# A SwiGLU second layer in 26 bilinear products instead of Strassen's 28, with hidden rows summed per four f tiles

## The chip, the core and the metric

One core of one Trainium2 chip runs the whole kernel. The metric is the device time of one execution in microseconds (us), median over runs; lower is better. All inputs and the output are fp32.

The engines in the text are TensorE (PE, matrix products), VectorE (DVE), ScalarE (ACT), GpSimd (POOL) and SyncE (SP, which here only issues DMAs). Each engine works through its own list of instructions strictly in order. POOL and SP both issue DMAs from such a list.

## The reference, cut

S = 2048 tokens, D = 1024, F = 3584, 32 heads of 32.

```python
xn = layernorm(x)
q, k, v = split_heads(xn @ wqkv)
phi = lambda t: where(t > 0, t + 1, exp(t)) + 1e-6
kv, z = einsum("bhsd,bhse->bhde", phi(k), v), phi(k).sum(s)
o = (phi(q) @ kv) / (phi(q) . z + 1e-6)
s = o @ wo
h = silu(xn @ w1) * (xn @ w3)            # 2048 x 3584
out = x + s * silu(h @ w2)               # w2 is 3584 x 1024
```

## The kernel before

**Products.** Every large product is cut into 2 x 2 blocks and computed with Strassen's 7 products of sums of blocks (`PRODUCTS`, L69). Each fp32 operand is split into a high and a low part (`split`, L92: ACT makes the high part at L96, DVE the low part at L97), and `mm3` (L101) multiplies a pair with three matmuls of 128x512 on L104 to L106.

**Stages.** The tokens are taken in two halves of 1024, h = 0 and h = 1. In each half come keys and queries, then the hidden layer: 14 pairs of f tiles (`half`, L785; one f tile is 128 of the 3584 columns), each with a gate and an up product (`gemm`, L547), 168 matmuls per pair. After the second half the attention product `attention` (`Segment`, L1146) makes s = o @ wo with a merged weight `wp`, in eight token groups m = 0..7, and stores s. Then the second layer h @ w2 follows (`Layer`, L1246) in five blocks of f (`FB`), its results added up in SBUF in `acc`, with silu, the multiplication by s and the addition of x in `finish` (L1402).

**Hidden rows.** `use_gate` (L874) puts silu(gate) into a 2 KB tile `sg`; `use_up` (L878) multiplies by up on DVE (L880) and stores the rows of h with a POOL DMA (L884). `sums` (L888) makes the four sums of blocks that Strassen needs for its left operands, with four POOL additions of 128x256 (`four_sums`, L863 to L867) per token chunk, into tiles `hs`, and stores them (L892) from POOL in h = 0 and from SP in h = 1. The `sg` tiles come from a pool of four places (`psg`), the `hs` tiles from `pc`.

**Jobs.** Side work is written as generators in a list `jobs`. `catch_up` (L530) advances the first of them by one step, at about six places per `gemm`; what is left when the hidden layer is issued is then run to its end (`for j, _ in jobs: run(j)` in `half`). Jobs use four shared 4 KB places (`job_tile`, L125). In h = 0 the jobs are `prepare_next` and 23 of the 28 sums of second-layer weights (`weight_sums`, L905: load 512 KB of w2, four POOL additions of 128x256 on L899 to L903, store to `wt_d`). In h = 1 the remaining five sums run on DVE during keys and queries, then `attention_work` (L1110): the divided queries `qd`, the merged weights `wp`, and more divisions.

**Into the attention product.** The first token group's raw left operands (`left`, L1328, with `first=True`) are put in job places: `r0q`, `r2q`, `r4q`, `r6q`, two operands each, loaded by SP from `qs_d` and split on ACT and DVE into `XA11s`, `XS2s` and so on. PE's first attention matmul, `B11s<-wp,XA11s`, needs the first of them.

The order of instructions on each engine is set by the framework's scheduler when the kernel is compiled. Names in the rows below: `h1_13_1` is the h tile of half 1, pair 13, second f tile; `hs1_6_20` holds sums of half 1, quad 6, product 20; `w2_5_1` is the loaded weight block of quad 5, column part 1, and `w2s5_1_0` the first tile of its sums. `DMAHW` and `DMASW` are lanes of SP's and POOL's DMA queues; a DMA that waits for a lane waits for the last DMA on it. The number at the end of each name counts buffers.

## Time and profile before

| what | value |
|---|---|
| time, three runs | 2308.01, 2309.46 (median), 2310.02 us |
| span of the profiled execution | 2307.8 us |
| median less span | 1.66 us |
| granted TensorE clock over the span | 1.000 |
| first matmul of the attention product, last of the hidden layer (they interleave) | 1611.68 and 1615.08 us from the span's start |
| first matmul of the second layer | 1768.39 us |
| busy share: PE, DVE, ACT, POOL | 99%, 77%, 40%, 27% |

The rows of a profile give, for each engine, source line and shape, how many instructions there were, how long they were busy and what the engine waited for before them. POOL's 27% is a mean over the span: it is busy in the two hidden stages and almost idle after 1640 us.

### The profile page before, as it was taken

Reading aid. Unit: us, or ns where it says so; the run is one execution under the profiler, and the core shown is the slowest. Engines: PE = TensorE matmul, PEld = TensorE weight load, DVE = VectorE, ACT = ScalarE, POOL = GpSimd, SP = SyncE. Lnnn points to the kernel's source line nnn. Section 1 sums busy time; section 2 is a strip of 40 time slices with the busy share of each in tenths; the row PEclk is TensorE's granted clock in tenths of the full one; section 3 lists DMA queues with packets and bytes.
Section 4 is the critical chain, followed back from the end, with each engine's and each line's share of the span. In section 5 each row is a group of like instructions: output and inputs, shape, how many; then the busy total and the mean of one; then the engine's idle time right before and its main releaser. Section 6 shows DMA issues by size and latency. Waiting matters only on the chain.

```text
span 2307.8 us, 31551 instructions
## 1 busy us (share of the span) xinstructions
PE 2285.8 (99%) x10752; PEld 1875.1 (81%) x10752; DVE 1769.3 (77%) x2870; ACT 927.4 (40%) x1653; POOL 624.3 (27%) x779
## 2 busy tenths in 40 slices
PE   7999999999999999999999999999999999999998
PEld 6888888888888887777888888888888888888887
DVE  8987888897876775667867788887745676767697
ACT  6555443423332555433333433334324634243443
POOL 2220524286854211001423345342310000000011
PEclk9999999999999999999999999999999999999999
DMA  6555556576659656886756667665756544654488
GB/s 238 182 181 177 184 170 192 164 242 210 215 182 333 214 178 215 274 255 195 225 183 191 192 196 213 203 213 167 239 171 194 160 141 139 197 158 149 147 272 255
DMA packets 346657, 461.90 MB, mean 200 GB/s; under 512 B 23184, under 2 KB 261776, under 8 KB 346384
## 3 DMA queue, kind: packets, MB, share of 16 engines
q1 hardware_dynamic: 311488, 348.72, 48.3%
q0 software_dynamic: 35008, 111.18, 15.0%
q8 instruction: 84, 1.38, 0.3%
q14 instruction: 77, 0.63, 0.1%
HBM read 297.27 MB, written 166.20 MB: 201 GB/s over the span
## 4 chain that ended last, share of the span: by engine, by line
PE 94%; DVE 3%; DMA 2%; issue 0%; ACT 0%; SPq 0%; DVEq 0%; ACTq 0%
PE aB L106 3%; PE aB L105 3%; PE aB L104 3%; PE g L104 2%; PE g L105 2%; PE g L106 2%; PE dB L106 2%; PE dB L105 2%; PE dB L104 2%; PE cB L105 1%; PE bB L105 1%; PE cB L106 1%; PE bB L106 1%; PE bB L104 1%; PE cB L104 1%; PE trk L645 1%
## 5 line engine op out<-in xcount | busy, mean ns | idle before, releaser
L884 POOL DMA_DIRECT2D h_d<-sg x112 | 82.6, 738 | 286.7 <-DVE sg L880 264.8
L1415 POOL DMA_DIRECT2D out<-acc x14 | 7.9, 562 | 484.7 <-DVE acc L1414 476.9
L97 DVE TENSOR_TENSOR xy<-xy,xy 128x512 fp32r<-128x512 f32 x112 | 72.9, 686 | 63.7 <-ACT xy L96 63.7
L1259 DVE TENSOR_TENSOR acc<-aB,acc 128x512 f32<-128x512 f32 x111 | 73.5, 687 | 57.3 <-PE aB L106 57.3
L96 ACT CAST xy<-xy 128x512 fp32r<-128x512 f32 x112 | 65.0, 620 | 101.5 <-PE g L106 62.1
L105 PE MATMUL g<-xy,xy 128*128 128x512 f32 x224 | 87.6, 391 | 0.2 <-DVE xy L97 0.2
L106 PE MATMUL g<-xy,xy 128*128 128x512 f32 x224 | 87.2, 390 | 0.0
L104 PE MATMUL g<-xy,xy 128*128 128x512 f32 x224 | 82.6, 398 | 0.0
L649 POOL DMA_DIRECT2D y_d<-y x48 | 34.6, 723 | 125.7 <-ACT y L673 70.4
L866 POOL TENSOR_TENSOR hs<-sg 128x256 f32<-128x256 f32 x56 | 59.7, 1065 | 0.0
L864 POOL TENSOR_TENSOR hs<-hs,sg 128x256 f32<-128x256 f32 x56 | 58.9, 1051 | 0.1
L1259 DVE TENSOR_TENSOR acc<-dB,acc 128x512 f32<-128x512 f32 x56 | 38.5, 688 | 21.1 <-PE dB L106 20.6
L104 PEld LDWEIGHTS g<-xy,xy 128*128 128x128 f32 x224 | 41.8, 188 | 14.2 <-issue 3.7
L867 POOL TENSOR_TENSOR hs<-sg,hs 128x256 f32<-128x256 f32 x56 | 51.0, 911 | 1.6
L1383 POOL DMA_DIRECT2D s_d<-s x32 | 17.3, 541 | 121.9 <-DVE s L1190 69.2
L863 POOL TENSOR_TENSOR hs<-sg,sg 128x256 f32<-128x256 f32 x56 | 49.6, 887 | 1.2
L105 PEld LDWEIGHTS g<-xy,xy 128*128 128x128 f32 x224 | 42.0, 188 | 9.7 <-DVE xy L97 1.0
L1028 POOL DMA_DIRECT2D qs_d<-qd x32 | 18.1, 564 | 115.9 <-DVE qd L1024 82.4
L106 PEld LDWEIGHTS g<-xy,xy 128*128 128x128 f32 x224 | 42.0, 188 | 8.8
L892 POOL DMA_DIRECT2D h_d<-hs x60 | 46.4, 774 | 3.9 <-POOL hs L867 2.4
L96 ACT CAST XA12B<-rA12B 128x384 fp32r<-128x384 f32 (+1 forms) x40 | 19.8, 494 | 63.4 <-PE aB L106 54.6
L805 POOL DMA_DIRECT2D pq_d<-pq x32 | 17.5, 548 | 99.0 <-DVE pq L639 98.9
(5327 smaller groups left out, 8196.2 us busy)
## 6 DMA issues: line engine op xcount, KB each, us to landing
h_d<-hs POOLq DMA_DIRECT2D x60, 256.0 KB, 3.1
h_d<-sg POOLq DMA_DIRECT2D x56, 256.0 KB, 3.7
w<-in_B_w SPq DMA_DIRECT2D x56, 256.0 KB
wt_d<-w SPq DMA_DIRECT2D x28, 512.0 KB
xy<-x_d SPq DMA_DIRECT2D x28, 512.0 KB
xy<-y_d SPq DMA_DIRECT2D x28, 512.0 KB
h_d<-hs SPq DMA_DIRECT2D x52, 256.0 KB
y_d<-y POOLq DMA_DIRECT2D x48, 256.0 KB, 3.2
```

What stands on the lines that cost most here:

```text
L96: nc.scalar.copy(out=hi, in_=src)
L97: return nc.vector.tensor_sub(out=lo, in0=src, in1=hi.bitcast(F32))
L104: nc.tensor.matmul(acc, lhsT=wh, rhs=ah, start=start, stop=False, skip_group_check=True)
L105: nc.tensor.matmul(acc, lhsT=wh, rhs=al, start=False, stop=False, skip_group_check=True)
L106: return nc.tensor.matmul(acc, lhsT=wl, rhs=ah, start=False, stop=stop, skip_group_check=True)
L863: e.tensor_add(out=s1, in0=a21, in1=a22)
L864: e.tensor_sub(out=s2, in0=s1, in1=a11)
L866: e.tensor_sub(out=s3, in0=a11, in1=a21)
L867: e.tensor_sub(out=s4, in0=a12, in1=s2)
L884: nc.gpsimd.dma_start(out=h_d[i][2 * h + c][:, 2 * n:4 * n + 2, k], in_=src)
L892: queue.dma_start(out=h_d[i][2 * h + c][:, 6 + 4 * e:10 + 4 * e, k], in_=o[e].rearrange("p (e s) -> p e s", s=P))
L1259: nc.vector.tensor_add(out=c[t, n], in0=src, in1=c[t, n])
```

## The change

**Second layer.** Instead of 28 products for a 4 x 4 x 2 block scheme (Strassen four times over) there are 26 (`CHAINS`, `TAKES`), over all of f at once: f is cut into 4 groups of 7 tiles, tokens into 4 tiles per chunk of 512, the output into 2 halves. Products that go to neighbouring outputs are chained in one PSUM bank. A step is one product and one token chunk: 104 steps of 7 f tiles x 3 = 21 matmuls of 128x512. Signs are carried by `NEGATED` right operands. The right operands are sums of four blocks of w2.

**Hidden sums.** The rows of h are now summed per quad of four f tiles. `early_sums` (after an even pair) issues 7 POOL additions or subtractions and 6 DMAs, `later_sums` (after an odd pair) 21 and 10, all of 128x256 elements. They are generators in `hsums`, one step per `catch_up`. All their DMAs are issued by POOL. The last quad's sum tiles are job places.

**Weight sums.** There are still 28 tasks, now one per quad t and column part, with 11 POOL operations each: 7 on 128x256 elements and 4 on 128x128. A task uses three job places (the loaded block `r`, and `o1`, `o2`) and three stores. 16 tasks run in h = 0; the other 12 are on POOL in h = 1, appended to the jobs behind `attention_work`, instead of five on DVE during keys and queries.

**Places.** Ten shared 4 KB places (`pb`) take the operands, the h tiles and the raw left operands, in place of eight of 4 KB and four of 2 KB.

The diff, cut:

```diff
+    CHAINS = [[7], [23, 6, 0], [21, 20, 18, 19], [10, 8, 3], [1, 25, 17], [24, 4, 13, 12], [22, 11, 16, 5], [14, 15, 9, 2]]
...
-    pb = era2.enter_context(tc.tile_pool(name="pb", bufs=8, side="right"))
-    psg = era2.enter_context(tc.tile_pool(name="psg", bufs=4, side="right"))
+    pb = era2.enter_context(tc.tile_pool(name="pb", bufs=10, side="right"))
...
     def catch_up(*marks):
 
+        if hsums and next(hsums[0], done) is done:
+            hsums.pop(0)
...
-            jobs.append((last_weight_sums(), True))
...
         jobs.append((attention_work(), False) if h else (next_work(), True))
+        if h:
+            jobs.append((last_weight_sums(), False))
...
         for j, _ in jobs:
             run(j)
         jobs.clear()
+        if h:
+            for j in hsums:
+                run(j)
+            hsums.clear()
...
         def use_up(n, c, src):
-            nc.vector.tensor_mul(out=sg[n, c], in0=src, in1=sg[n, c])
...
+            a = tiles[2 * odd + n][:, c]
+            nc.vector.tensor_mul(out=a, in0=src, in1=a)
+            if (n, c) == (1, 0):
+                hsums.append((later_sums if odd else early_sums)(h, t, dict(tiles), last))
...
+    def later_sums(h, t, tiles, last):
+        q = quarter(tiles)
+
+        def pair(p):
+            return sums_tile(f"hs{h}_{t}_{p}", praw if last else None)
+
+        both, t3, t1 = pair(24)
+        add(t3, q["1b"], q["1d"])
+        take(t1, q["0c"], q["3c"])
+        store_both(h, t, 24, both)
...
+            e.tensor_sub(out=o1[:, 0:2], in0=some(r, 0, 6), in1=some(r, 1, 6))
+            e.tensor_add(out=o1[:, 2:4], in0=some(r, 0, 5), in1=some(r, 2, 5))
+            e.tensor_add(out=o1[:, 4:6], in0=r[:, 2:4], in1=o1[:, 0:2])
+            e.tensor_sub(out=o1[:, 6:8], in0=r[:, 4:6], in1=o1[:, 0:2])
+            store(0, o1)
+            yield True
+            e.tensor_sub(out=o2[:, 0:2], in0=some(r, 0, 3), in1=some(r, 4, 3))
+            e.tensor_sub(out=o2[:, 2], in0=o1[:, 2], in1=o1[:, 3])
+            e.tensor_sub(out=o2[:, 3], in0=o1[:, 2], in1=r[:, 6])
+            e.tensor_sub(out=o2[:, 4:6], in0=some(r, 2, 3), in1=o1[:, 5:7])
+            yield True
+            e.tensor_sub(out=o2[:, 6:8], in0=some(o1, 4, 3), in1=r[:, 3:5])
+            store(8, o2)
+            e.tensor_add(out=r[:, 0], in0=r[:, 1], in1=o2[:, 1])
+            e.tensor_add(out=r[:, 1], in0=o2[:, 0], in1=o2[:, 1])
+            store(16, r[:, 0:2])
             yield True
...
-    NOW = len(WSUMS) - 5
+    WSUMS = [(t, part) for t in range(NQ) for part in range(4)]
+    NOW = 16
...
-        yield from go_on([weight_sums(*w, nc.vector) for w in WSUMS[NOW:]])
+        yield from go_on([weight_sums(*w) for w in WSUMS[NOW:]])
...
+    for s, (i, c) in enumerate(STEPS):
+        p = ORDER[i]
+        if s + 4 < len(STEPS):
+            left_ask(s + 4)
+        if s + 2 < len(STEPS):
+            left_split(s + 2)
+        fetch_for(s + 2)
...
+        b, L = banks[c], lefts[s]
+        for t in range(NQ):
+            R = rights[i, t]
+            mm3(b, (L[:, 0, t], L[:, 1, t]), (R[:, 0], R[:, 1]), p in OPENS and t == 0, t == NQ - 1)
```

**How the order moves, first place: the end of the hidden layer on POOL.** Before, these are POOL's last rows of the hidden layer, up to the first store of s:

```order
L866 TENSOR_TENSOR hs1_13_0_1_14006<-sg1_13_00_13832 128x256 [waits DMAHW7_49]
L892 DMA h_d22_3_106<-hs1_13_1_1_13982 128x4x128 [waits DMASW5_49,Pool_49]
L864 TENSOR_TENSOR hs1_13_0_0_14005<-hs1_13_0_0_14005,sg1_13_00_13832 128x256 [waits Pool_49]
L892 DMA h_d22_2_105<-hs1_13_0_0_14005 128x4x128 [waits DMASW6_49,Pool_49]
L867 TENSOR_TENSOR hs1_13_0_1_14006<-sg1_13_10_13871,hs1_13_0_0_14005 128x256
L892 DMA h_d22_2_105<-hs1_13_0_1_14006 128x4x128 [waits DMASW7_49,Pool_49]
L1383 DMA s_d0_140<-s0_00_14169 128x512 [waits DMASW0_49,DVE_49]
```

In the changed kernel POOL's list reads, from the store of the last pair's first rows on:

```order
L925 DMA h_d1_88<-h1_13_1_14045 128x2x128 [waits DMASW2_49,DVE_49]
L1050 TENSOR_TENSOR w2s4_3_1_14153<-w2_4_3_14053,w2s4_3_0_14152 128x256 [waits Pool_49]
L1052 TENSOR_TENSOR w2s4_3_1_14153<-w2s4_3_0_14152,w2_4_3_14053 128x256
L1055 TENSOR_TENSOR w2_4_3_14053<-w2s4_3_1_14153 128x128 [waits Pool_49]
L1041 TENSOR_TENSOR w2s5_0_0_14229<-w2_5_0_14147 128x256 [waits DMAHW1_49,DMAHW3_49,DMAHW0_49,Pool_49]
L1042 TENSOR_TENSOR w2s5_0_0_14229<-w2_5_0_14147 128x256 [waits DMAHW2_49]
L1047 TENSOR_TENSOR w2s5_0_1_14230<-w2_5_0_14147 128x256 [waits DMAHW2_49]
```

Behind the store of `h1_13_1` stand the last three operations of task `w2_4_3` and then the eight whole tasks `w2_5_0` to `w2_6_3`, 91 operations in all (58 on 128x256, 33 on 128x128), in the order of the code; only then, apart from three of them, the last quad's later sums `hs1_6`. The first operation of a task (L1041) waits, by its lanes, for its loads and for the store of the preceding task's second tile, whose place it takes.

The last quad's sums end with these rows, the stores of `hs1_6_13` and `hs1_6_20` among them; between the last weight sum and this point stand 13 operations and 5 stores:

```order
L916 TENSOR_TENSOR hs1_6_6_14455<-hk1_6_13995,h1_13_0_14077 128x256 [waits DMASW3_49]
L919 TENSOR_TENSOR hs1_6_20_14451<-h1_13_1_14045,hs1_6_20_14451 128x256 [waits Pool_49]
L929 DMA h_d1_88<-hs1_6_13_14446 128x4x128 [waits DMASW7_49,Pool_49]
L919 TENSOR_TENSOR hs1_6_6_14455<-hs1_6_6_14455,hs1_6_20_14451 128x256 [waits Pool_49]
L929 DMA h_d1_88<-hs1_6_20_14451 128x4x128 [waits DMASW0_49,Pool_49]
```

**Second place: SP's loads for the attention product.** Before, the load of the first left operands follows the weight load of hidden pair 13's gate:

```order
L425 DMA wg1_13__13536<-in_B_w1 128x8x256 [waits DMAHW6_49,DVE_49]
L1340 DMA r0q_0_14013<-qs_d0_128 128x512 [waits DMAHW7_49,DMASW3_49,DMASW0_49]
L1340 DMA r0q_0_14013<-qs_d0_128 128x512 [waits DMAHW0_49]
L892 DMA h_d22_3_106<-hs1_11_1_0_13394 128x4x128 [waits DMAHW1_49,Pool_49]
L892 DMA h_d22_3_106<-hs1_11_1_1_13395 128x4x128 [waits DMAHW2_49,Pool_49]
```

Now it stands behind all stores of the weight sums:

```order
L1039 DMA wt_d6_102<-w2_6_2_14371 128x2x128 [waits DMAHW5_49,Pool_49]
L1039 DMA wt_d6_102<-w2s6_3_0_14413 128x8x128 [waits DMAHW6_49,Pool_49]
L1039 DMA wt_d6_102<-w2s6_3_1_14414 128x8x128 [waits DMAHW7_49,Pool_49]
L1039 DMA wt_d6_102<-w2_6_3_14392 128x2x128 [waits DMAHW0_49,Pool_49]
L1394 DMA r0q_0_14469<-qs_d0_103 128x512 [waits DMAHW1_49,DMAHW4_49,DMASW5_49,DMAHW7_49,DMASW0_49,Pool_49]
L1394 DMA r0q_0_14469<-qs_d0_103 128x512 [waits DMAHW2_49]
```

The load of `r0q` moved from the middle of the last hidden pairs to behind the last task's third store, which waits for POOL's last weight sum. Its job place is that of the last quad's sums `hs1_6_7` and `hs1_6_20`: it waits for their stores (lanes DMASW5 and DMASW0).

**Third place: ACT in the hidden layer of h = 0.** Before, ACT's silu of pair 10 writes into the small tiles `sg`:

```order
L877 ACTIVATE sg0_10_11_5269<-c22g0_10__5250 128x512 [waits DMASW6_49,DVE_49,Pool_49]
L877 ACTIVATE sg0_10_00_5291<-ag0_10__5190 128x512 [waits DMASW4_49,PE_49,Pool_49]
L96 CAST T4u0_10__5294<-wu0_10__5018 128x512 [waits Activation_49]
L96 CAST B22u0_10__5314<-wu0_10__5018 128x512 [waits PE_49,Activation_49]
L877 ACTIVATE sg0_10_01_5312<-c21g0_10__5249 128x512 [waits DMASW5_49,DVE_49,Pool_49]
```

In the changed kernel the same stretch reads:

```order
L579 COPY uu0_10__5523<-au0_10__5524 128x512
L903 ACTIVATE h0_10_0_5462<-ag0_10__5319 128x512 [waits DMASW6_49,Pool_49]
L903 ACTIVATE h0_10_0_5462<-c21g0_10__5400 128x512 [waits DVE_49]
L103 CAST T4u0_10__5465<-wu0_10__5141 128x512 [waits DMASW1_49,Pool_49]
L103 CAST B22u0_10__5490<-wu0_10__5141 128x512 [waits PE_49,Activation_49]
```

The silu of `h0_10_0` and the weight operand `T4u0_10` now take places that earlier h tiles held, and wait for POOL's last sum from those tiles and for their stores.

501 lines of the change are left out of this document (270 added, 231 removed).

## The prediction

> **What bounds the kernel now.** I read the page's totals and its chain first. Columns of the first row: busy time, share of the span, instructions.
>
> ```profile
> span 2307.8 us, 31551 instructions
> PE 2285.8 (99%) x10752; PEld 1875.1 (81%) x10752; DVE 1769.3 (77%) x2870; ACT 927.4 (40%) x1653; POOL 624.3 (27%) x779
> ...
> PE 94%; DVE 3%; DMA 2%; issue 0%; ACT 0%; SPq 0%; DVEq 0%; ACTq 0%
> ```
>
> PE is busy for all but 22 us of the span, and 94% of the chain that ends last runs through it. So the kernel takes what its matmuls take, plus any time in which PE is made to wait. The second view cuts the span into stretches: busy time and instructions of PE, weight loads, DVE, ACT and POOL, then granted clock, DMA share, GB/s.
>
> ```profile
> 500.00:600.00 100.00, 100.00 (x443) 82.84 (x442) 82.70 (x97) 31.82 (x54) 78.29 (x90) 1.00 0.65 208
> 1590.00:1610.00 20.00, 20.00 (x90) 16.57 (x89) 13.99 (x23) 12.81 (x24) 0.00 (x0) 1.00 0.42 134
> 1635.00:1750.00 115.00, 114.20 (x501) 93.64 (x500) 63.30 (x98) 35.39 (x60) 14.61 (x27) 1.00 0.64 197
> 1750.00:2205.00 455.00, 455.00 (x2009) 376.86 (x2008) 327.58 (x589) 185.49 (x375) 2.71 (x5) 1.00 0.53 162
> 2205.00:2300.00 95.00, 95.00 (x421) 78.69 (x420) 84.85 (x148) 36.63 (x69) 20.16 (x28) 1.00 0.91 272
> ```
>
> PE is full in the hidden layer (500:600) and in the second layer (1750:2205). One matmul takes 455.00/2009 = 0.2265 us of PE. POOL, on the other hand, is 78% busy in the weight-sum stretch of h = 0, at rest just before the hidden layer ends, and nearly idle in the second layer. DMA is close to full only in the last 95 us.
>
> The third view is the timeline at the end of the hidden layer, PE rows and then POOL rows: start, duration, line.
>
> ```profile
> 1611.45 0.39 PE L106 MATMUL eu__13898<-A,T4u__13931 128*128 128x512 f32 x1
> 1611.68 0.39 PE L104 MATMUL B11s<-wp,XA11s 128*128 128x512 f32 x1
> ...
> 1612.59 0.39 PE L104 MATMUL du__13897<-S,B22u__13949 128*128 128x512 f32 x1
> ```
>
> ```profile
> 1610.63 0.77 POOL L884 DMA_DIRECT2D h_d<-sg  x1 [24.89 <-DVE sg L880]
> ...
> 1617.98 0.75 POOL L863 TENSOR_TENSOR hs<-sg,sg 128x256 f32<-128x256 f32 x1
> 1618.67 0.74 POOL L866 TENSOR_TENSOR hs<-sg 128x256 f32<-128x256 f32 x1
> 1619.37 0.74 POOL L864 TENSOR_TENSOR hs<-hs,sg 128x256 f32<-128x256 f32 x1
> ```
>
> The attention product starts without a gap: its first matmul stands even ahead of the last 12 of the hidden layer. POOL had waited 24.89 us for work and stored the last pair's first rows at 1610.63.
>
> **The change part by part: the matmuls.** The second layer had 28 products x 4 x 21 = 2352 matmuls and has 26 x 4 x 21 = 2184. The 168 that go were all on PE, the path: 168 x 0.2265 = **-38.1 us**.
>
> Does the new layer stay bound by PE? A step has 21 matmuls, 4.76 us. These rows give the work beside it:
>
> ```profile
> L1259 DVE TENSOR_TENSOR acc<-aB,acc 128x512 f32<-128x512 f32 x111 | 73.5, 687 | 57.3 <-PE aB L106 57.3
> L97 DVE TENSOR_TENSOR XS1B<-rS1B,XS1B 128x384 fp32r<-128x384 f32 x32 | 17.6, 551 | 2.9 <-ACT XS1B L96 2.9
> L96 ACT CAST xy<-xy 128x512 fp32r<-128x512 f32 x112 | 65.0, 620 | 101.5 <-PE g L106 62.1
> L97 DVE TENSOR_TENSOR xy<-xy,xy 128x512 fp32r<-128x512 f32 x112 | 72.9, 686 | 63.7 <-ACT xy L96 63.7
> ```
>
> DVE per step: a left low part of 896 elements, about 0.686 + 384 x (0.686 - 0.551)/128 = 1.09 us; 182/104 right low parts x 0.686 = 1.20; 88/104 additions x 0.687 = 0.58; and the finishing products and additions, 50/104 x 0.69 = 0.33. That is 3.2 of 4.76 us. ACT, with a cast of about 0.9, 1.75 casts x 0.62 and small copies, has about 2.4. Neither becomes the bound. Loads are 896 KB a step, 193 GB/s, against 162 now; where outputs are finished, in products 21 to 25 of the list, another 0.7 MB a step makes about 335, while the last stretch now moves 272 GB/s at a DMA share of 0.91. Over 20 steps that costs between nothing and 95 x (335 x 0.91/272 - 1) = 11 us, hidden in part by loads made ahead. The last addition before silu now goes through DVE (0.69). Together **+4 us**, between 1 and 15.
>
> **The end of the hidden layer.** This is the large term. POOL's list has, behind the store of `h1_13_1`, 91 weight-sum operations, then the last quad's sums. SP loads `r0q` only behind the last weight-sum store, and into the place that `hs1_6_20` leaves. So PE's first attention matmul is queued behind all that POOL work. When can it run? POOL's prices:
>
> ```profile
> L866 POOL TENSOR_TENSOR hs<-sg 128x256 f32<-128x256 f32 x56 | 59.7, 1065 | 0.0
> L899 POOL TENSOR_TENSOR w<-w 128x256 f32<-128x256 f32 x23 | 22.4, 972 | 35.7 <-DMA w<-in_B_w 35.3 <-PE dg__4268 L106 0.4
> L903 POOL TENSOR_TENSOR w<-w 128x256 f32<-128x256 f32 x23 | 20.8, 915 | 0.8
> L903 POOL TENSOR_TENSOR wo<-wo 128x512 f32<-128x512 f32 x4 | 6.1, 1537 | 0.2
> L899 POOL TENSOR_TENSOR wo<-wo 128x512 f32<-128x512 f32 x4 | 5.7, 1427 | 48.0 <-DMA wp_d<-wo 45.4 <-ACT wo L1088 2.6
> L291 POOL TENSOR_TENSOR B11k__307<-w0k__226,B11k__307 128x512 fp32r<-128x512 f32 x1 | 1.3, 1296 | 0.0
> L892 POOL DMA_DIRECT2D h_d<-hs x60 | 46.4, 774 | 3.9 <-POOL hs L867 2.4 <-POOL hs L864 1.5
> ```
>
> An operation on 128x256 advances POOL by 0.70 us when it is quick (1617.98, 1618.67, 1619.37 above), and by about 0.96 on the mean of such rows (0.915 to 1.065, less the overlap). No row shows 128x128 on POOL. From 0.74 and 1.296 at 512 elements, the slope gives 0.74 - 0.28 = 0.46, about 0.43 of advance; from the two means at 512 and at 256, 0.60 and 0.74, so 0.66. I keep both ends. Up to the store of `hs1_6_20` there are 58 + 3 + 13 = 74 operations on 128x256, 33 on 128x128 and 6 DMA issues: 74 x 0.70 + 33 x 0.43 + 6 x 0.77 = 70.6 us quick, 74 x 0.96 + 33 x 0.66 + 6 x 0.77 = 97.4 us on the mean. Which rate? These rows show who disturbs whom:
>
> ```profile
> 1631.88 1.22 DVE L97 TENSOR_TENSOR XA11s<-rA11q,XA11s 128x512 fp32r<-128x512 f32 x1
> 1633.02 0.68 DVE L97 TENSOR_TENSOR XS2s<-rS2q,XS2s 128x512 fp32r<-128x512 f32 x1
> ```
>
> ```profile
> 1631.35 1.20 POOL L867 TENSOR_TENSOR hs<-sg,hs 128x256 f32<-128x256 f32 x1
> 1632.84 0.78 POOL L892 DMA_DIRECT2D h_d<-hs  x1 [0.30 <-POOL hs L867]
> ```
>
> A DVE subtraction of the same shape takes 1.22 us beside a POOL sum and 0.68 after it, and POOL's own 1.20 stands against 0.74. DVE has splits to do until about 1635, as now, and then nothing, since it waits for the same loads. So I take the mean rate for the first 25 us, in which 18 us of quick work is done, and the quick one for the rest: 77.5 us.
>
> In each of the eight tasks the first operation waits until the preceding task's 512 KB store has landed. The nearest rows:
>
> ```profile
> 559.07 1.91 POOL L903 TENSOR_TENSOR w<-w 128x256 f32<-128x256 f32 x2
> 568.88 0.74 POOL L899 TENSOR_TENSOR w<-w 128x256 f32<-128x256 f32 x1 [7.89 <-DMA w<-in_B_w]
> ...
> h_d<-hs POOLq DMA_DIRECT2D x60, 256.0 KB, 3.1
> ```
>
> There, POOL waited 7.89 us for a 512 KB store and then a 512 KB load, about 3.9 each; less one small operation that POOL still does meanwhile, 3.5. Eight times: 28 us, between 0 and 28. Then the last store has to land (3.1), `r0q` to be loaded (about the same) and split (0.62 + 0.69): 7.5 us. So attention starts at 1610.63 + 0.77 + 77.5 + 28 + 7.5 = 1724.4, on the scale of before; at the quick rate without store waits at 1689.5; at the mean rate throughout at 1744.3. PE has done its hidden layer at 1611.68 + 12 x 0.2265 = 1614.4. PE therefore stands still for **+110 us**, between 75 and 130. Nothing covers it: the PE has no other work, and the attention product behind it is as long as before.
>
> A rule on the rate. The lowest advance in the rows is 0.70. The Trainium skill ("GPSIMD Engine Reference", 1 and 2.1) has GpSimd sharing its SBUF interfaces with VectorE, which these rows bear out (1.20 against 0.74), and a floor for two inputs of 2.5 cycles per element at 1.2 GHz; that is an estimate of 0.53 us for 256 elements, by which the 107 operations would take 48 us instead of 66 and the sum would be some 20 us less. The trace has no such instruction; the row decides.
>
> A rule on the restart. The granted clock is 1.00 in every stretch above, in which PE hardly pauses. The same skill ("TensorE: Matmul & The Clock Gate", Part 1) says that an idle PE drops to half clock and needs about 3.4 us of work to return; by that the sum would be about 1.7 us more. No run here shows it yet.
>
> **The hidden layer of h = 0.** The 16 weight-sum tasks now run in three quads (pairs 6 to 11), 6, 5 and 5. Per quad PE has 2 x 168 x 0.2265 = 76.1 us. POOL has 28 sums and 16 DMAs of about 0.75 (L892 above), and five tasks: 63 operations on 128x256, 20 on 128x128. At the mean rates 60.5 + 13.2 + 12 = 85.7 us, 9.6 more than PE; with six tasks 95. At the quick rates 44 + 8.6 + 12 = 65 us, which fits. DVE is as busy there (82.70 of 100 us) as in the rows that gave the mean rates, so POOL falls behind by 9.6 + 9.6 + 19 = 38 us at worst. Lateness reaches PE by the h tiles: ACT waits for a place until POOL has made its sums, and behind that silu are queued ACT's next weight operands, for which PE waits. Even now:
>
> ```profile
> ACT sg L877 <- POOL w L902: 2.0, 2, 1.0
> ```
>
> Some lateness is free, since places are ten. I take **+20 us**, between 0 and 40. In h = 1 POOL has only 28 sums, 16 stores and the stores of `qd` per quad, which fits.
>
> **The sum** on the profiled execution: 2307.8 - 38.1 + 110 + 20 + 4 = 2403.7 us of span, and with the 1.7 by which the median of 2309.46 exceeds it, **2405 us**.
>
> **Rivals.** (1) *The light stall.* POOL runs at its quick rate, the store waits hide, and h = 0 keeps up: 2309.5 - 38.1 + 75 + 1 = 2347. For it speaks that DVE falls idle; against it that L1041's wait names the store. Chance 0.2. (2) *The heavy one*: mean rates to the end and all of the lateness: 2309.5 - 38.1 + 130 + 40 + 15 = 2456. For it, that no POOL group quoted above averages under 0.915 us; against it the idle DVE. Chance 0.1. (3) *Faster.* The backlog passes while PE still has work: POOL, alone on SBUF once DVE waits, does its 107 operations at a rate that no row shows. PE's stall then has to stay under 38 - 4 = 34 us, that is, the 70.6 us of quick work would have to shrink to about 29, some 0.24 us per operation against 0.70; fully hidden, the time is 2309.5 - 38.1 + 4 = 2275. The profile speaks against it. Chance 0.07. The forecast has the remaining 0.63.
>
> A difference of 0.2%, 4.6 us, is what a measurement can tell from none. Faster by more: 0.07; within: 0.02, between rivals 1 and 3; slower: 0.91. The range, from a little under the light stall to a little under the sum of all upper ends: 2340 to 2450 us.
>
> **What would show it.** Right: PE idle for about 110 us between the last `du` and `B11s`, POOL busy there with L1041 to L1055 and waiting for `wt_d` stores; the second layer at about 495 us from its first matmul to the last; PE waits for ACT in h = 0, pairs 8 to 12. Wrong: PE going on within 30 us of the hidden layer, or a second layer with PE gaps.

## The result: 2487 us, 7.7% slower, and the profile after

The changed kernel takes 2487.34 us (median of four runs, 2482.65 to 2492.41) against 2309.61 us (2308.01 to 2310.02). The ratio is 1.0772, with a 95% interval of 1.0755 to 1.0789. The forecast was 2405 us: the direction was right, but the loss is 178 us and not 95, and the time lies above the range.

The page's totals, PE's and POOL's slices and the granted clock of the profiled execution (2484.81 us, span 2483.0):

```profile
span 2483.0 us, 30861 instructions
PE 2280.4 (92%) x10584; PEld 1856.8 (75%) x10584; DVE 1714.3 (69%) x2534; ACT 926.3 (37%) x1554; POOL 914.0 (37%) x1211
...
PE   6999999998999999999999999994069999999999
...
POOL 2221425489996411003445555566730100001010
PEclk8999999999999999999999999997589999999999
```

PE stands still for 203 us now, 22 before. One hole is seen at once, in slices 28 and 29, where POOL works. The rest does not show in tenths. Stretches show it (columns as in the prediction):

```profile
500.00:600.00 100.00, 89.69 (x378) 72.12 (x377) 71.05 (x81) 26.25 (x46) 90.62 (x116) 0.96 0.67 196
600.00:700.00 100.00, 94.82 (x401) 76.89 (x401) 82.59 (x82) 27.72 (x49) 93.84 (x117) 0.97 0.61 183
...
1700.00:1800.00 100.00, 9.68 (x43) 7.70 (x41) 24.35 (x34) 13.67 (x24) 66.59 (x105) 0.56 0.73 217
```

In the hidden layer of h = 0, PE was full with 443 matmuls per 100 us; now it has 378 and 401, and POOL is over 90% busy. The second layer, from its first matmul to its last, is the one stretch without a loss:

```profile
1982.00:2477.00 495.00, 494.96 (x2184) 409.59 (x2182) 303.17 (x415) 228.45 (x340) 19.10 (x27) 1.00 0.71 233
```

The list of PE's waits (us in total, times, longest) names the single large one and then many of 1 to 5 us, on `bu`, `dg` and `du` of the hidden pairs:

```profile
PE B11s L109 <- ACT XA11s L103: 112.0, 1, 112.0
...
PE tS L291 <- DVE S L303: 10.2, 1, 10.2
PE dg__2919 L109 <- DVE c22g__2966 L616: 5.0, 1, 5.0
PE bu__14159 L109 <- ACT T2u__14126 L103: 4.4, 1, 4.4
PE bu__10163 L109 <- ACT T2u__10119 L103: 3.7, 1, 3.7
```

The chain that ends last, in the hole (start, us, what; one weight-sum task, then the end):

```profile
1767.61 0.72 POOL w2s L1041
1768.32 0.68 POOL w2s L1042
...
1772.92 0.73 POOL w2s L1052
1773.66 3.21 DMA wt_d<-w2s
1777.04 0.72 POOL w2s L1041
...
1814.68 0.73 POOL hs L919
1815.42 0.70 POOL h_d L929
1817.50 0.62 POOL hs L919
1818.12 2.78 DMA r0q<-qs_d
1820.98 0.63 ACT XA11s L103
1821.65 0.79 PE B11s L109
```

A task takes 9.43 us, 3.21 of them the store for which the next one waits. Nine of the twelve tasks of h = 1 run in the hole, then the last quad's sums, and only then the load of `r0q`.

**Where the time went.** Both kernels run nearly the same matmuls up to the second layer, so the lateness of one of them, after less before, can be read at marks: the first gate product of a pair, the first row product, the first attention matmul and so on. What a stage adds to the lateness is its loss. For the changed kernel: opening +11.0; hidden layer of h = 0, pairs 0 to 6 +15.7, pairs 7 to 13 +34.1; keys, queries and row products of h = 1 +2.2; hidden layer of h = 1, pairs 0 to 6 +9.2, pairs 7 to 13 +22.0; transition to attention +115.8; attention +3.4; second layer -38.1. The sum is 175.3 us, and the spans differ by 175.2.

### The profile page after: what moved, and what is told of

Its sections match the earlier page's. It is cut to its first block, busy times and chain, and to the rows that moved or that the text cites. A ratio compares the mean times of both kernels' runs of the same rounds, so it can differ in the third digit from the quotient of the medians.

```text
span 2483.0 us, 30861 instructions
## 1 busy us (share of the span) xinstructions
PE 2280.4 (92%) x10584; PEld 1856.8 (75%) x10584; DVE 1714.3 (69%) x2534; ACT 926.3 (37%) x1554; POOL 914.0 (37%) x1211
## 3 DMA queue, kind: packets, MB, share of 16 engines
q0 software_dynamic: 37952, 120.09, 15.1%
## 5 line engine op out<-in xcount | busy, mean ns | idle before, releaser
L109 PE MATMUL o<-w,l 128*128 128x512 f32 x728 | 283.3, 389 | 0.0
L111 PE MATMUL o<-w,l 128*128 128x512 f32 x728 | 283.3, 389 | 0.0
L110 PE MATMUL o<-w,l 128*128 128x512 f32 x728 | 283.3, 389 | 0.0
L103 ACT CAST l<-lr 128x896 fp32r<-128x896 f32 (+1 forms) x106 | 98.6, 932 | 202.6 <-PE o L111 106.2
L104 DVE TENSOR_TENSOR l<-lr,l 128x896 fp32r<-128x896 f32 (+1 forms) x106 | 113.4, 1072 | 82.3 <-ACT l L103 81.6
L109 PEld LDWEIGHTS o<-w,l 128*128 128x128 f32 x728 | 136.7, 188 | 28.5
L110 PEld LDWEIGHTS o<-w,l 128*128 128x128 f32 x728 | 136.7, 188 | 28.3
L111 PEld LDWEIGHTS o<-w,l 128*128 128x128 f32 x728 | 136.7, 188 | 28.3
L1612 DVE TENSOR_TENSOR acc<-o,acc 128x512 f32<-128x512 f32 x64 | 43.7, 688 | 88.9 <-PE o L111 88.9
L109 PE MATMUL B11s<-wp,XA11s 128*128 128x512 f32 x4 | 2.2, 549 | 112.0 <-ACT XA11s L103 112.0
L925 POOL DMA_DIRECT2D h_d<-h x70 | 50.5, 722 | 112.8 <-DVE h L907 71.5
L929 POOL DMA_DIRECT2D h_d<-hs x112 | 85.7, 766 | 4.1 <-POOL hs L919 3.0
L664 POOL DMA_DIRECT2D y_d<-y x48 | 35.2, 742 | 124.1 <-ACT y L688 69.8
L104 DVE TENSOR_TENSOR w<-wr,w 128x512 fp32r<-128x512 f32 x98 | 63.0, 684 | 1.9 <-ACT w L103 1.8
```

The lines of the kernel that those rows point to most:

```text
L103: nc.scalar.copy(out=hi, in_=src)
L104: return nc.vector.tensor_sub(out=lo, in0=src, in1=hi.bitcast(F32))
L109: nc.tensor.matmul(acc, lhsT=wh, rhs=ah, start=start, stop=False, skip_group_check=True)
L110: nc.tensor.matmul(acc, lhsT=wh, rhs=al, start=False, stop=False, skip_group_check=True)
L111: return nc.tensor.matmul(acc, lhsT=wl, rhs=ah, start=False, stop=stop, skip_group_check=True)
L664: nc.gpsimd.dma_start(out=y_d[h][:, :, YS.index(n), pair], in_=t.rearrange("p (t d) -> p t d", d=P))
```

## The experiments

The theory after the result: POOL's queue makes the hole, places held by the h tiles and POOL's lateness make the losses in the hidden layers, and the opening is a matter of its own. Rivals were that the hidden losses come from the weight sums alone, from DVE and ACT (their operands come later whatever POOL does), and that the hole is set by something other than POOL's arithmetic. Each kernel below was executed once, beside one execution of the kernel before on the same chip (2307.5 to 2309.5 us). They are compared stage by stage in one table; us lost against the kernel before:

| kernel | time | opening | h=0, 0-6 | h=0, 7-13 | keys, rows | h=1, 0-6 | h=1, 7-13 | transition | attention |
|---|---|---|---|---|---|---|---|---|---|
| changed | 2484.81 | 11.0 | 15.7 | 34.1 | 2.2 | 9.2 | 22.0 | 115.8 | 3.4 |
| e1 x laid late | 2467.38 | -1.7 | 14.9 | 33.1 | 3.3 | 9.1 | 20.9 | 115.0 | 1.3 |
| e2 sums in the rows | 2471.12 | 10.7 | 15.3 | 35.5 | 25.0 | 19.8 | 33.4 | 56.5 | 3.5 |
| e3 two tiles held | 2468.64 | 10.7 | 4.5 | 35.2 | 4.3 | 4.5 | 20.9 | 114.5 | 2.6 |
| e4 no weight sums | 2383.04 | 11.6 | 15.6 | 0.0 | 0.9 | 9.9 | 23.5 | 50.2 | -0.1 |
| e5 no tile held | 2477.09 | 9.4 | 7.4 | 41.8 | 3.5 | 1.8 | 22.5 | 114.9 | 4.3 |
| e6 two steps | 2489.68 | 10.3 | 15.4 | 38.9 | 2.3 | 75.3 | 37.9 | 34.1 | 4.0 |
| e7 three edits | 2441.70 | -1.5 | 14.7 | 33.1 | 2.2 | 70.0 | 46.2 | 0.5 | 5.0 |
| e8 eleven places | 2473.06 | -2.1 | 0.1 | 52.0 | 1.8 | 91.5 | 53.1 | -0.9 | 6.1 |
| e9 loads freed | 2375.37 | -1.8 | 15.1 | 32.9 | 2.4 | 6.9 | 18.6 | 3.6 | 26.2 |
| e10 no divisions | 2477.36 | 10.2 | 14.9 | 36.2 | 17.7 | 1.0 | 89.1 | 33.9 | 2.9 |
| e12 sums on both | 2381.43 | -1.5 | 14.2 | 41.1 | 0.9 | 9.2 | 21.5 | 3.6 | 21.0 |
| e13 twelve tasks | 2388.45 | -1.6 | 12.1 | 23.9 | 1.3 | 9.3 | 22.7 | 3.7 | 36.1 |
| e14 side work after | 2690.28 | 9.6 | 15.5 | 46.1 | 13.9 | -14.3 | 4.2 | 339.7 | 3.8 |
| e15 no row sums | 2432.97 | 9.8 | 15.0 | 38.4 | 3.1 | -0.2 | -0.7 | 92.2 | 3.9 |
| e16 neither | 2645.51 | 10.1 | 14.6 | 33.2 | 15.5 | -20.3 | -0.9 | 317.5 | 3.9 |

How far to trust a cell: kernels whose h = 0 is not edited read 33 to 39 us in its pairs 7 to 13, once 46. Differences under about 6 us there say nothing.

**The opening: e1.** SP's own rows in the changed kernel, then in e1:

```profile
14.34 0.55 SPq L228 DMA_DIRECT2D w0k__206<-in_A_wqkv  x1
14.93 6.40 SPq L1440 DMA_DIRECT2D out<-in_A_x  x7
25.86 0.38 SPq L228 DMA_DIRECT2D w1k__396<-in_A_wqkv  x1
27.75 3.48 SPq L228 DMA_DIRECT2D w1k__447<-in_A_wqkv  x1
```

```profile
13.94 0.56 SPq L228 DMA_DIRECT2D w0k__206<-in_A_wqkv  x1
21.85 0.37 SPq L228 DMA_DIRECT2D w1k__396<-in_A_wqkv  x1
25.71 0.37 SPq L228 DMA_DIRECT2D w1k__447<-in_A_wqkv  x1
```

The diff had taken a wait away from `lay_x`, and the scheduler put seven copies of x to the output ahead of the second weights' loads. DVE and PE waited for these:

```profile
46.56 0.69 DVE L471 TENSOR_TENSOR w0k__206<-w1k__447,w0k__206 128x512 f32<-128x512 f32 x1 [11.21 <-DMA w1k__447<-in_A_wqkv]
```

```diff
-        nc.sync.dma_start(out=out[rows, :], in_=x[rows, :])
+        with tc.issue_after(loads[-1].ins):
+            nc.sync.dma_start(out=out[rows, :], in_=x[rows, :])
```

> The seven copies of x into the output wait again for a second-layer load, so that they can't be issued in the opening. Theory (each loss has its own cause: copies in the opening 11 us, held places in both hidden layers 82 us, the queue of weight sums 112 us): the delay at the first queries' product falls from 11.0 us to under 1 us, nothing else changes by over 3 us, about 2475 us in all. Rival (the opening's wait comes from the order of the shared places): the delay stays at 11 us and the time at about 2487 us.

Measured: opening -1.7 instead of +11.0, all other stages as they were. The copies ahead of the loads are the whole 11 us.

**The hole: e2, e4, e6, e7, e9.** e2 runs the twelve weight-sum tasks in the row products, ahead of the divisions:

```diff
             jobs.append((all_denominators(), False))
+            jobs.append((last_weight_sums(), False))
...
-        if h:
-            jobs.append((last_weight_sums(), False))
```

> The twelve weight sums of the second half are put ahead of the denominators, so that they run during the row products. Theory of the POOL queue: behind the last pair's first store POOL has only the last quad's 21 sums and 10 stores, so PE stands still for 20 to 35 us instead of 112 us before the attention product, about 2405 us in all. Rival (the load for the attention product is late for SP's or the DMA's sake): PE still stands still for over 60 us.

Measured: transition 56.5, so without one weight sum left, half of the hole stays: divisions, their loads and stores, and the last quad's sums, all still ahead of `r0q`. The tasks cost 23 us in the row products, and the hidden layer of h = 1 loses 22 us more. Moving the work was worth 14 us. The stall lies between the 20 to 35 us of the theory and the over 60 us of its rival: the queue is the cause, but the weight sums are only half of it.

e4 keeps the tasks' loads and stores but leaves out their sums (a part of the computation):

```diff
-            e.tensor_sub(out=o1[:, 0:2], in0=some(r, 0, 6), in1=some(r, 1, 6))
...
-            store(16, r[:, 0:2])
+            for i in (0, 8):
+                yield True
+                nc.sync.dma_start(out=wt_d[t][:, i:i + 8, cols], in_=r)
...
+            nc.sync.dma_start(out=wt_d[t][:, 16:18, cols], in_=r[:, 0:2])
```

> All 28 weight-sum tasks keep their loads and their three stores, but leave out the 11 POOL operations, so the sums of w2 are missing from the result. Theory: the loss in the hidden layer of the second half (33 us) and that of the first half's pairs 2 to 6 (16 us) stay, the first half's pairs 7 to 13 fall from 34 us to 10 to 20 us, and the stall before the attention product to 20 to 35 us; about 2385 us. Rival (weight sums on POOL are behind all losses in the hidden layers): both hidden layers lose under 10 us in all, about 2330 us.

Measured: 50.2 in the transition, where 20 to 35 had been expected and the tasks' loads and stores still stand ahead of `r0q`; and in the hidden layer of h = 0 the 34 us of pairs 7 to 13 are gone. The same 100 us as above, in e4:

```profile
600.00:700.00 100.00, 100.00 (x443) 82.81 (x442) 71.57 (x97) 31.48 (x52) 52.11 (x61) 1.00 0.74 227
```

PE is full again, POOL at 52%. The weight sums on POOL are the whole cause of pairs 7 to 13 in h = 0, where 10 to 20 us had been expected to stay, and of none of the loss in h = 1's hidden layer. How POOL's lateness reaches PE is seen in the changed kernel's rows of ACT, DVE and PE:

```profile
561.63 0.60 ACT L903 ACTIVATE h<-ag__4572 128x512 f32<-128x512 f32 x1 [11.24 <-POOL hs L916]
563.28 3.40 DVE L104 TENSOR_TENSOR T4u__4718<-wu__4394,T4u__4718 128x512 fp32r<-128x512 f32 x1 [10.57 <-ACT T4u__4718 L103]
566.73 0.79 PE L111 MATMUL eu__4815<-A,T4u__4718 128*128 128x512 f32 x1 [2.70 <-DVE T4u__4718 L104]
```

ACT's silu waits 11.24 us for POOL's sums, the operand `T4u` is queued behind it on ACT, DVE's part of it then takes 3.40 us beside POOL's sums where 0.68 is usual, and PE waits for that.

e6 takes two job steps per call in h = 1; e7 adds e1's wait, and gives the last quad's sums tiles of their own pool instead of job places:

```diff
                 if next(job, None) is None:
                     jobs.pop(0)
+                elif twice and next(job, None) is None:
+                    jobs.pop(0)
...
-            return sums_tile(f"hs{h}_{t}_{p}", praw if last else None)
+            return sums_tile(f"hs{h}_{t}_{p}", None)
```

> In the second half's hidden layer two steps of the side work are taken where one was, so that none is left when the last pair ends. Theory (the stall of 112 us is the side work left over, behind which the last quad's sums and the attention product's first loads are queued): PE stands still for 20 to 35 us, the time of the last quad's sums alone; the second half's hidden layer loses 10 to 25 us more, since the weight sums now run beside it; about 2420 us. Rival (the 46 to 53 us that were left without weight sums there are the price of loads through the job places as such): over 45 us.

> The changed kernel with three edits: copies of x behind a second-layer load, two steps of side work in the second half's hidden layer, and the last quad's sums in small tiles in place of job places, so that the attention product's first loads wait for no sum. Theory: opening -1.7 us against the kernel before, both hidden layers 80 to 105 us late in all as now with weight sums in both, the stall before the attention product under 8 us, second layer 495 us; 2360 to 2385 us. Rival (the attention product's start has another late operand behind these): the stall stays above 20 us, over 2390 us.

Measured: the hole shrinks to 34.1 in e6, where only the last quad's sums stand ahead of `r0q`, and is gone in e7 (0.5). But the hidden layer of h = 1 loses 113 and 116 us instead of 31, where 10 to 25 us more had been expected. One stretch of it in e7, and its largest PE wait:

```profile
1300.00:1400.00 100.00, 74.25 (x301) 58.67 (x300) 66.31 (x130) 16.97 (x31) 53.57 (x69) 0.88 0.60 189
```

```profile
PE dg__11120 L109 <- ACT B22g__11198 L103: 17.6, 1, 17.6
```

No engine is full there. The work was moved under PE's matmuls and came back as many waits; what makes each of them was not taken apart.

e9 goes the other way. It leaves the work where it is, and frees the loads: the first token group's raw operands take the shared places instead of job places, with e1's wait and the last quad's sums out of the job places.

```diff
-        return left(m, lambda n: qs_d[m][:, LEFT.index(n)], ND // 2, "q", m == 0)
+        return left(m, lambda n: qs_d[m][:, LEFT.index(n)], ND // 2, "q")
```

> The copies of x behind a second-layer load; the last quad's sums in small tiles; and the attention product's first left operands loaded into shared places like all later ones, not into job places. The weight sums stay where they are, eight tasks behind the last pair. Theory (the stall was not POOL's work itself but that PE's first operands were queued behind it): POOL still sums for about 90 us after the hidden layer, now beside the attention product; PE stands still under 15 us there and under 15 us more within the attention product; hidden layers as in the changed kernel; 2360 to 2390 us. Rival (SP's list holds the loads of later token groups behind stores that wait for POOL): the stalls move into the attention product, over 40 us there, 2400 us or more.

Measured: transition 3.6 instead of 115.8, 2375.37 us in all, the best of the versions that compute everything. The nine tasks run beside the attention product, which then takes 23 us longer than in the changed kernel, between the under 15 us of the theory and the over 40 us of the rival. Attention before, in the changed kernel and in e9, each from its first matmul to the second layer's first:

```profile
1612.00:1768.00 156.00, 155.20 (x683) 127.58 (x682) 90.01 (x133) 49.21 (x86) 28.53 (x44) 1.00 0.62 192
```

```profile
1822.00:1982.00 160.00, 155.50 (x674) 126.75 (x674) 73.00 (x116) 43.73 (x74) 15.85 (x31) 0.99 0.48 156
```

```profile
1690.00:1872.00 182.00, 164.54 (x669) 129.54 (x669) 116.54 (x142) 55.16 (x95) 113.17 (x161) 0.93 0.83 264
```

So the hole is the order of two queues and a place, not an amount of work that PE must wait for: with the loads freed, 26 of the 116 us remain. e9 is still 2.9% slower than the kernel before.

**Held places: e3, e5, e8.** In pairs 0 to 6 of h = 0 no wait of ACT for POOL shows; ACT's waits for POOL's sums, as the one at 561.63 us above, all lie in pairs 7 to 13 or later. Whether held places cost anything ahead of them was asked by three runs. e3 makes the later sums read the second pair's two tiles only, so the first two come free a pair earlier (it sums other blocks than the reference needs); e5 replaces all inputs after the first two sums by tiles that are kept anyway, and stores two rows early (other blocks too); e8 is e7 with an eleventh shared place, paid for by two of the six small ones.

```diff
-        q = quarter(tiles)
+        q = quarter({k: tiles[2 + k % 2] for k in tiles})
```

> The later sums read the odd pair's h tiles in place of the even pair's, with the same number and shape of operations and stores, so that the even pair's two places come free one pair earlier; the sums are then of other blocks. Theory of held places: the loss in the hidden layer of the second half falls from 33 us to under 15 us, and that of the first half's pairs 2 to 6, ahead of any weight sum, from 16 us to under 8 us; about 2450 us in all. Rival (POOL is late or slows DVE by its sums): both stay as they are, 2487 us.

```diff
+        q = {n: kept[n[0] in "13"] for n in q}
...
+        store_rows(h, t, 22, q["0d"])
+        q = {m + k: kept[m in "13"] for m in "0123" for k in "abcd"}
```

> All but the first two of a quad's 28 sums read a kept tile in place of the h tiles, with the same number and shape of operations and stores, so that h tiles give their places back as soon as their own rows are stored; the sums are then of other blocks. Theory of held places (it asks for more than the run before, in which two of four tiles were still held): the loss in the second half's hidden layer falls from 31 to 33 us to under 8 us, that of the first half's pairs 2 to 6 from 16 us to under 4 us, and the 34 us of its pairs 7 to 13 stay within 10 us, since POOL's work is the same; about 2440 us. Rival (the second half's loss has to do with POOL's sums or the attention product's side work, not with places): it stays above 20 us, about 2465 us.

```diff
-    pc = ctx.enter_context(tc.tile_pool(name="pc", bufs=6))
+    pc = ctx.enter_context(tc.tile_pool(name="pc", bufs=4))
...
-    pb = era2.enter_context(tc.tile_pool(name="pb", bufs=10, side="right"))
+    pb = era2.enter_context(tc.tile_pool(name="pb", bufs=11, side="right"))
```

> The three edits and eleven shared 4 KB places in place of ten, paid with two of six small 2 KB tiles. Theory of held places: the first half's pairs 2 to 6 lose under 10 us where they lost 16, the second half's hidden layer 5 to 15 us less than with ten; 10 to 25 us under the run with the three edits. Rival (places are not short, small tiles are): as long or longer than that run.

Measured in pairs 0 to 6, where no weight sum runs yet in h = 0: 15.7 falls to 4.5, 7.4 and 0.1, and in h = 1, 9.2 to 4.5 and 1.8. Held places are that loss; e8 shows it best, with all sums of the changed kernel and one place more. Why e5, which frees more, leaves more than e3 in h = 0 stays open. Pairs 7 to 13 don't answer to them (35.2 and 41.8 against 34.1; 20.9 and 22.5 against 22.0), and so h = 1 as a whole, 25.4 us in e3 and 24.3 in e5, misses the under 15 and under 8 us that the theory asked for: the rival was right there. In h = 0's pairs 7 to 13, e5's silu waits up to 12.6 us for the stores of h, which POOL issues, where the changed kernel's waited for POOL's sums. e8 gives its gain back: with four small places its pairs 7 to 13 lose 52 us in h = 0 against 33 in e7, and h = 1 28 us more. The total is 31 us worse.

**The engine of the weight sums: e12, e13.** Both are e9 with one line changed: every second task of h = 0 on DVE, or twelve tasks in h = 0 instead of sixteen.

```diff
-        yield from go_on([weight_sums(*w) for w in WSUMS[:NOW]])
+        yield from go_on([weight_sums(*w, nc.vector if i % 2 else nc.gpsimd) for i, w in enumerate(WSUMS[:NOW])])
```

> As the run with free loads, and every second of the first half's sixteen weight sums on DVE in place of POOL. Theory (POOL is overfull in pairs 6 to 12): eight tasks fewer are some 75 us of POOL, eight more some 32 us of DVE, which has 18 us free in 100: the 34 us of pairs 7 to 13 fall to 5 to 20 us. Rival (DVE is as short as POOL there): 30 us or more.

```diff
-    NOW = 16
+    NOW = 12
```

> As the run with free loads, with twelve weight sums in the first half in place of sixteen, the other sixteen in the second. Theory: four tasks fewer take some 38 us from POOL where it is 38 us too full, so the 34 us of pairs 7 to 13 fall under 10 us, and four more tasks beside the attention product cost under 10 us there: 20 to 35 us under the run with free loads. Rival (the backlog then outlasts the attention product and holds the second layer's operands): no gain, stalls at the second layer's start.

Measured: e12's pairs 7 to 13 lose 41.1 against e9's 32.9. DVE is no help, against the 5 to 20 us expected: it is 71 and 83% busy there itself in the two stretches shown at first. e13 loses 23.9, 9 us less, but attention and the second layer pay 10 + 9.5 us more for the four tasks that now come late; 20 to 35 us less than e9 had been expected, and 13 more came. No place that was tried, row products, hidden layers, attention or DVE, takes these sums for nothing.

**The hidden layer of h = 1, pairs 7 to 13: e10, e14, e15, e16.** This loss had outlived the places (e5) and the weight sums (e4). e10 leaves out the arithmetic of the divided queries, a part of the computation:

```diff
-            nc.vector.scalar_tensor_tensor(t[:, :2], t[:, :2], 1e-6, t[:, 2:], op0=ALU.add, op1=ALU.mult)
-            for _ in four_sums(t[:, 0], t[:, 1], t[:, 2], t[:, 3], nc.vector):
-                pass
```

> The changed kernel without DVE's five operations per division of the queries (their product and four sums), with all their loads and stores, so the queries are not divided. Theory: the loss of 22 us in the second half's pairs 7 to 13, which neither held places nor weight sums explain, comes from DVE, which has those operations to do just when the up operands are made late: it falls under 8 us. Rival (DVE has room, the loss is in the order of ACT's and DVE's lists alone): over 15 us stay.

Measured: 89.1 us instead of 22, which says nothing on the divisions themselves. With them gone the jobs moved up, and all twelve weight-sum tasks ran in these pairs; in the changed kernel three did:

```profile
L1052 POOL TENSOR_TENSOR w2s<-w2s,w 128x256 f32<-128x256 f32 x12 | 10.6, 885 | 0.0
```

So three runs were made that change the load and not its place. e14 begins nothing of h = 1's side work before the layer's end; e15 stores the unsummed tiles instead of the sums of h in h = 1, with as many stores; e16 does both. e15 and e16 thus leave out the sums of h = 1's rows.

```diff
+        if h:
+            jobs.append((attention_work(), False))
+            jobs.append((last_weight_sums(), False))
         for j, _ in jobs:
             run(j)
```

> The changed kernel, but of h = 1's side work (the divisions and the eight left weight sums) nothing is begun before the hidden layer's last product; all of it then runs in one piece ahead of attention. What is asked is only the loss in the hidden layer of h = 1, which in the changed kernel is 9 us over pairs 0 to 6 and 22 us over pairs 7 to 13. Theory A (the divisions and their loads, beside the rows' sums, make ACT and DVE late for the operands): the 22 us fall below 6. Theory B (the rows' own sums on POOL and their stores are enough): the 22 stay above 16. The 9 us of pairs 0 to 6 were put down to places held by h tiles and should stay at 6 to 10 by either. The stall ahead of attention must grow, from 112 us to 250 or more, so the whole is later, about 2600 us.

```diff
     def later_sums(h, t, tiles, last):
+        if h == 1:
+            yield from plain(h, t, tiles, [[24, 10], [7], [0], [13], [20], [6], [18], [16]])
+            return
         q = quarter(tiles)
```

> The changed kernel, but in h = 1 the sums of h are left out: the same number of stores goes out from the unsummed tiles, and POOL computes nothing for them. This leaves out part of the computation. Theory A (divisions make the operands late): 16 us or more of pairs 7 to 13's 22 stay. Theory B (the rows' sums on POOL): below 6 stay. Pairs 0 to 6 fall from 9 to 4 or less by both, since the tiles come free as soon as they are stored. If either part alone takes most of the 22 away, the two together are the cause, and neither alone.

> The changed kernel with both edits: no side work in the hidden layer of h = 1, and no sums of h on POOL there (which leaves out part of the computation). If side work and sums are together the whole cause, pairs 7 to 13 lose 0 to 3 us against the kernel before, and pairs 0 to 6 no more than 4. If 16 or more of the 22 us stay, the cause is neither, but the shared places of the operands or the order of ACT's list.

Measured in pairs 7 to 13: 22.0 falls to 4.2 without the side work and to -0.7 without the row sums. Each theory's own test came out for it, so neither alone is the cause: it is the two together. Pairs 7 to 13 before, in the changed kernel, in e14 and in e15:

```profile
1348.00:1615.00 267.00, 267.00 (x1180) 221.08 (x1179) 221.68 (x376) 91.92 (x156) 108.80 (x130) 1.00 0.65 199
```

```profile
1420.00:1709.00 289.00, 274.36 (x1175) 224.14 (x1175) 239.37 (x373) 83.43 (x146) 176.65 (x225) 0.98 0.61 188
```

```profile
1419.00:1690.00 271.00, 266.81 (x1175) 219.99 (x1174) 170.00 (x244) 78.66 (x136) 108.70 (x145) 1.00 0.28 89
```

```profile
1414.00:1681.00 267.00, 266.85 (x1177) 220.41 (x1175) 197.92 (x363) 81.44 (x143) 91.24 (x124) 1.00 0.69 203
```

DVE has nearly the same work before, after and in e15, 363 to 376 instructions, and takes 0.590, 0.642 and 0.545 us for one, as POOL is busy for 109, 177 and 91 us. The divisions' own rows, before, in the changed kernel and in e15:

```profile
L866 DVE TENSOR_TENSOR qd<-qd 128x128 f32<-128x128 f32 x23 | 6.5, 281 | 0.0
```

```profile
L883 DVE TENSOR_TENSOR qd<-qd 128x128 f32<-128x128 f32 x23 | 11.2, 488 | 0.4
```

```profile
L883 DVE TENSOR_TENSOR qd<-qd 128x128 f32<-128x128 f32 x23 | 6.6, 289 | 0.4
```

DMA traffic is not the difference: e15 moves 203 GB/s, the changed kernel 188. More sums on POOL make DVE's instructions longer, and DVE, with divisions in its list, then has the sums of the weights late, of which the operands for PE are made: PE's waits in these pairs are mostly on `T2u`, as for `bu__14159` in the list at first. This link through DVE is read from rows and waits; no run changed DVE's speed alone. In pairs 0 to 6, e14 and e16 show gains of 14 and 20 us that are none: side work puts small matmuls of its own on PE there (the pairs take 289.9 us before, against 267.5 for pairs 7 to 13), which these two move away. Less those 22 us, e14 still loses about 8, the held places, and e16 about 2. Why the row products lose 12 us more in e14 and e16 stays open.

## Why the prediction was right or wrong

**The matmuls: right.** 168 fewer, -38.1 us; the second layer took 494.96 us where about 495 was forecast, and no stage of it waits. The +4 us for heavier steps came to nothing.

**The hole: right in mechanism; that the size agrees to 2 us is in part luck.** PE waited 112.0 us at `B11s`, against 110. The prices held: a store that the next task waits for took 3.2 us (3.5 taken), 128x256 on POOL advanced by 0.68 when DVE was idle (0.70 taken), 128x128 by 0.41 (0.43 taken). But from POOL's store of the last pair's first rows to `B11s` 102.9 us passed where the sum has 113.8, 10.9 less; and that store, forecast 3.8 us ahead of the end of PE's hidden layer, came 9.3 us behind it (1718.77 us), 13 more. The two cancel. The mean of 128x128 over the whole kernel, beside a busy DVE for the most part, is between the two ends, 0.46 and 0.66:

```profile
L1048 POOL TENSOR_TENSOR w2s<-w2s 128x128 f32<-128x128 f32 x28 | 17.7, 633 | 0.0
...
L1054 POOL TENSOR_TENSOR w<-w,w2s 128x128 f32<-128x128 f32 x28 | 15.0, 534 | 0.0
```

The floor of 0.53 us for 256 elements, an estimate from the Trainium skill ("GPSIMD Engine Reference", 1 and 2.1), was not reached even with DVE at rest; the trace's quick row was the better price. From 128 to 256 elements the advance grows by 0.27 us, half of that floor, but 0.14 us stand beside it that do not grow. What that page says of the shared interface the runs bear out on DVE's side (281 against 488 ns above).

**The hidden layer of h = 0: too small, +20 against +49.8.** POOL's lateness by five tasks a quad was put at 38 us at worst, and 34.1 came, by the path that was named, ACT's silu behind POOL's sums (11.24 us at 561.63). PE's own waits there are on DVE more than on ACT, where the prediction's sign was waits for ACT. The step that failed is "Some lateness is free, since places are ten. I take +20 us". The ten places are no reserve: the h tiles hold them from the first quad on, and pairs 0 to 6 lose 15.7 us without a weight sum in sight. The table of places, how many are held and for how long, was never drawn up.

**The hidden layer of h = 1: the failed step.** "In h = 1 POOL has only 28 sums, 16 stores and the stores of `qd` per quad, which fits." It does fit: POOL is busy for 177 of 289 us. But the prediction had quoted a DVE subtraction that took 1.22 us beside POOL and 0.68 alone, used it for POOL's price, and did not put it on DVE's side in the stage where DVE had 83% to do. It cost 22 us there, and the places 9.

**The opening: not looked at, +11.0.** The diff's `lay_x` lost a wait, and the order of SP's list in the first 30 us would have shown the seven copies. The prediction took the stages outside its three places as unchanged.

**The sum.** Forecast +95.9 of span; measured 175.2. Missing are 11.0 (opening), 29.8 (h = 0), 31.2 (h = 1), 5.8 (transition) and 2.2 (rows), less 0.6: attention lost 3.4, and the 4 for the second layer's steps did not come. The heavy rival, 2456 us, priced the hole too high, and the opening and h = 1 at nothing as well.

**The restart of the clock: right for one stall, and there were many.** The 1.7 us that the Trainium skill's rule ("TensorE: Matmul & The Clock Gate", Part 1) gave for the hole are what the rows show:

```profile
1821.65 0.79 PE L109 MATMUL B11s<-wp,XA11s 128*128 128x512 f32 x1 [111.97 <-ACT XA11s L103]
...
1825.10 0.39 PE L109 MATMUL B11s<-wp,XA11s 128*128 128x512 f32 x1
```

Eight matmuls start within these 3.45 us, where 1.81 would do; 1.6 us are lost. But the hidden layers' stalls have the same echo, as the last section shows, and there it was not counted.

## What to carry to other kernels

When side work moves to another engine, price it on every engine that shares memory with it, in the stage where that one is busiest; "it fits" on its own engine is half of the answer. Draw up who holds each shared buffer and for how long, and read the whole order of every queue that the diff moves, the first microseconds too. A large hole behind a queue may be worth little work and much order: freeing a few loads took 112 us of it away and gave 23 back, while moving the work itself brought 26 us at most (e7 against e1).

## What the runs showed of the hardware

PE's pitch halves after short stalls already. After the 5 us wait at `dg__2919` PE's rows read (start, duration):

```profile
344.70 0.79 PE L109 MATMUL dg__2919<-S,B22g__2865 128*128 128x512 f32 x1 [4.95 <-DVE c22g__2966 L616]
...
349.56 0.63 PE L111 MATMUL dg__2919<-S,B22g__2865 128*128 128x512 f32 x1
349.98 0.58 PE L111 MATMUL au__3060<-A,B11u__2889 128*128 128x512 f32 x1
350.40 0.39 PE L109 MATMUL au__3060<-A,B11u__2889 128*128 128x512 f32 x1
```

Matmuls follow each other at 0.43 us for 5.7 us, instead of 0.227, and the granted clock of that stretch is 0.50. Over the changed kernel 90 matmuls start 0.41 to 0.45 us after the one ahead of them, in the kernel before none: some 18 us of the loss are no waits at all, but their echo. The Trainium skill ("TensorE: Matmul & The Clock Gate", "Why this matters for your kernels") warns of gaps over about 3 us between bursts; the trace agrees, with slow stretches of 3.0 to 6.1 us after gaps of 3.1 to 5.3 between two starts in the hidden layers, while gaps of 2.1 to 2.6 us left the pitch as it was, and so did one of 3.3 (`bu__13127`).

POOL's sums lengthen DVE's instructions by more than a tenth on the mean of a stage (0.642 us against 0.545 in e15), and the mean of one group by 1.7 times (281 and 488 ns), though neither engine is full: 83% and 61% in that stretch. Single instructions are hit far harder. This subtraction takes 0.68 us alone:

```profile
719.63 5.67 DVE L104 TENSOR_TENSOR T2u__6022<-wu__5841,T2u__6022 128x512 fp32r<-128x512 f32 x1 [0.76 <-ACT T2u__6022 L103]
```

POOL makes seven sums without a pause meanwhile, from 719.77 to 724.64 us, each in 0.73 to 0.74, and begins an eighth. In the changed kernel 26 DVE operations on two tiles of 128x512 take 2 to 5.7 us, and POOL is busy beside each of them for 87% of that time or more; in e16, which has neither sums of h nor side work in pairs 7 to 13 of h = 1, no DVE instruction there takes over 0.70. On POOL's side the same operation advances by 0.68 us with DVE idle and by up to 1.15 beside it (1694.50 and 1695.65 us).
